# Attention scores as single float32 products from q and k as loaded, the last 64 keys as a chunk of their own, value products in two halves

## Chip, cores and metric

The kernel runs on one core of one Trainium2 chip. The metric is the device time of one execution in microseconds; lower is better. The time before is the median of three runs, and one further execution was profiled.

## What is computed

Sigmoid attention over 4 batches of 12 heads, 448 positions and 64 dimensions, whose output feeds two feed-forward layers with 1792 tokens:

```python
scores = scale * np.matmul(q, k.transpose(0, 1, 3, 2)) - np.log(S)   # S = 448, scale = 1 / 8
attn = 1.0 / (1.0 + np.exp(-scores))
out = np.matmul(attn, v)                       # (4, 12, 448, 64) -> x: (1792, 768)
xn = x / sqrt(mean(x * x) + 1e-06) * rms_g
y = (silu(xn @ w_gate) * (xn @ w_val)) @ w_out     # 768 -> 1536 -> 768
h = y @ w_in2                                      # 768 -> 2048
result = (h - tanh(h)) @ w_out2                    # 2048 -> 768
```

All inputs are float32.

## The kernel before, in words

Heads are worked on in 24 pairs (6 pairs in each of 4 batches). The two heads of a pair lie one above the other on the 128 partitions, 64 rows each, as 64 is the head's dimension. The 448 keys of a head are cut into chunks of 128, 128, 128 and 64.

`pair_load` (L444) brings a pair's q and k (with 4 to 8 transfers on SP's queue, L457) and its v (L466, or L476 and L477 with a fill of zeros on POOL at L471). `pair_prep` (L481) then splits q and k: a copy (L488, recorded at the helper's L278) makes a high part of type float32r, and a subtraction (L489) the low part. `scores` (L500) multiplies, for each chunk and each head, high by high, low by high and high by low (the matmul at L512); head 0 lies in rows 0 to 63 of the array and head 1 in rows 64 to 127. The sum comes out in a PSUM bank for each chunk and head. `sigmoid` (L521) takes each bank through ScalarE into SBUF (L522). `pair_qk` (L527) is called twice for a pair, for the chunks 0 and 1 and for 2 and 3. The short chunks of both heads are put into one tile of 128 rows.

`pair_av` (L541) multiplies with the values: for three chunks and two heads a float32 matmul (L551) whose heads lie in different columns of the array, and one matmul over the whole array (L555) for the short chunks of both heads at once, against a v tile in which the other head's rows are zero. `pair_end` (L561) copies the sum out of PSUM, and `x_end` (L567) squares it (L569) and adds it up (L576) for the norm.

After attention the kernel runs the two feed-forward layers for batches 0 and 1 and then for 2 and 3, as products of float32r parts (L768 and L803). Some of the first of these products are put between attention units of the last batches, with Silu (L712) on ScalarE.

The order is not written out by hand. Each step is added to a list with its engines, a cost for each, its reads, its writes and, for transfers, a time until they land. `Plan.issue` (L81) then simulates the engines with these costs: among the steps that can finish within 300 ns of the soonest it takes the one that was added first (some later work has its rank put back), and every engine gets its steps in the order of the simulated starts. Steps of the stream "attention" keep their order on TensorE. Buffers belong to pools with a cap for each kind: 74 `unit` tiles of 128 x 448 (L243), nine `wt` tiles for weights (L245: `raw` up to 3, `op` up to 6, `whl` and `again` up to 3), three `vs` tiles for v, and eight PSUM banks. `get_ready` (L817) prepares the next pair and loads the one behind it. Before the first scores TensorE runs 16 matmuls on zeros (L285, called at L839).

Of the kernel before, what the change touches and what calls it, by code (L numbers as in the profile page):

```python
# [8 lines left out]
F32 = mybir.dt.float32  # L9
F32R = mybir.dt.float32r  # L10
# [49 lines left out]
class Plan:  # L60
# [153 lines left out]
def tile_sigmoid_attention_moe_moe(  # L214
# [25 lines left out]
    dram_p = ctx.enter_context(tc.tile_pool(name="spill", bufs=1, space=DRAM))  # L240

    plan = Plan({
        "unit": (N_UNIT, {"moe": N_MOE, "s": 14, "qk": 8, "qkr": 4, "acc": 6, "st": 4, "sum": 6, "x": 16, "xr": 4, "tmp_m": 6, "tmp_a": 4, "sq": 3, "rstd": 2,  # L243
                          "xs": 42, "tmp_s": 4, "tmp_x": 4}),
        "wt": (N_WT, {"raw": N_RAW, "whl": 3, "again": 3, "op": 6}),  # L245
        "cv": (N_CV, {"cv": N_CV}),
        "vs": (3, {"vs": 3}),
        "ps": (8, {"mm": 6, "at": 8, "av": 2, "nm": 1, "m2": 8}),
# [3 lines left out]
    def slot(kind, pool, shape, dt, tag):  # L252
        return Slot(kind, lambda: pool.tile(shape, dt, tag=tag, name=tag))
# [4 lines left out]
    def unit(kind, dt=F32):  # L258
        return slot(kind, unit_p, [P, S], dt, "unit")
# [8 lines left out]
    def act(n, psum=False, ptr=False):  # L268
        return {"ACT": ((155 if psum else 195) + n / 1.2, False)}
# [7 lines left out]
    def copy(engines, to, of, reads, writes):  # L277
        add(engines, lambda e: (nc.scalar.copy if e == "ACT" else nc.vector.tensor_copy)(to(), of()), reads, writes)  # L278
# [159 lines left out]
                lambda: two(g[1], 0, ("S3", "S4")), lambda: two(g[1], 1, ("A22",))]  # L438


    qkr_t, vs_t, pair_t, a_t, av_t = {}, {}, {}, {}, {}
    xs, sqs, rcs, rstd, spilled = {}, {}, {}, {}, {}

    def pair_load(b, p):  # L444
        if (b, p) in qkr_t or (b, p) in pair_t:
            return
        t = qkr_t[b, p] = {w: unit("qkr") for w in "kq"}

        def load(w, lo, hi, key):

            for i in range(2):
                rows = slice(i * D, (i + 1) * D)
                of = qkt[b * H + 2 * p + i][rows]
                at = lo + S * (w == "k")
                if w == "k" and lo == 3 * P and b < PAIRED:
                    at += i * D
                add({"SP": (1.4 * (hi - lo), False)}, lambda e, of=of, rows=rows, at=at: nc.sync.dma_start(  # L457
                    out=t[w].tile[rows, lo:hi], in_=of[:, at:at + hi - lo]), [], [t[w][key, lo, i]], after=2000)

        for w, lo, hi in (("k", 0, P), ("q", 0, S), ("k", P, 3 * P), ("k", 3 * P, S)) if (b, p) == (0, 0) else (  # L460
                ("k", 0, 3 * P), ("k", 3 * P, S), ("q", 0, S)) if b < PAIRED else (("k", 0, S), ("q", 0, S)):
            load(w, lo, hi, "t")
            t.setdefault(w + "in", []).extend(t[w]["t", lo, i] for i in range(2))
        v = vs_t[b, p] = slot("vs", vs_p, [P, 4, 2, D], F32, "vs")
        if b < PAIRED:
            add({"SP": (700, False)}, lambda e: nc.sync.dma_start(out=v.tile, in_=vp[b * HP + p]), [], [v["t", i] for i in range(2)], after=2000)  # L466
            return

        def fill(e):
            for i in range(2):  # L470
                nc.gpsimd.memset(v.tile[(1 - i) * D:(2 - i) * D, 3, i, :], 0.0)  # L471

        add({"POOL": (250, True)}, fill, [], [v["t", 0], v["t", 1]])
        for i in range(2):
            def two(e, i=i, of=vt[(b - PAIRED) * H + 2 * p + i], rows=slice(i * D, (i + 1) * D)):
                nc.sync.dma_start(out=v.tile[:, :3, i, :], in_=of[:, :3])  # L476
                nc.sync.dma_start(out=v.tile[rows, 3, i, :], in_=of[rows, 3])  # L477

            add({"SP": (900, False)}, two, [], [v["t", i]], after=2000)

    def pair_prep(b, p):  # L481
        t = qkr_t.pop((b, p))
        f = pair_t[b, p] = {w: unit("qk", F32R) for w in ("kh", "qh", "kl", "ql")}

        def part(w, lo, hi, to):
            h, l, r = f[w + "h"], f[w + "l"], t[w]
            of = [x for x in t[w + "in"] if lo <= x[1][1] < hi]
            copy({**act(hi - lo), **dve(hi - lo, fast=True)}, lambda: h.tile[:, lo:hi], lambda: r.tile[:, lo:hi], of, [h[to]])  # L488
            add({**pool(hi - lo), **dve(hi - lo, psum=False)}, lambda e: ENG[e].tensor_sub(  # L489
                l.tile[:, lo:hi], r.tile[:, lo:hi], h.tile[:, lo:hi].bitcast(F32)), [*of, h[to]], [l[to]])  # L490

        if (b, p) == (0, 0):
            part("k", 0, P, 0)
            part("q", 0, S, 0)
            part("k", P, S, 1)
        else:
            for w in "kq":
                part(w, 0, S, 0)

    def scores(b, p, cs):  # L500

        f = pair_t[b, p]
        ps = {(i, c): bank("at") for c in cs for i in range(2)}
        key = (lambda c: min(c, 1)) if (b, p) == (0, 0) else (lambda c: 0)

        def run(e):
            for c in cs:
                n = min(P, S - c * P)
                for w, q in (("kh", "qh"), ("kl", "qh"), ("kh", "ql")):
                    for i in range(2):  # L510
                        rows = slice(i * D, (i + 1) * D)
                        nc.tensor.matmul(  # L512
                            ps[i, c].tile[:n, :S], lhsT=f[w].tile[rows, c * P:c * P + n], rhs=f[q].tile[rows, :],
                            start=(w, q) == ("kh", "qh"), stop=q == "ql")

        add({"PE": (3 * len(cs) * MM + 200, False)}, run,
            [x for c in cs for x in (f["kh"][key(c)], f["kl"][key(c)])] + [f["qh"][0], f["ql"][0]],
            [x["t"] for x in ps.values()], stream="attention")
        return ps

    def sigmoid(ps, n, to, at=0, key="t"):  # L521
# [3 lines left out]


    def pair_qk(b, p, cs):  # L527
        ps = scores(b, p, cs)
        for c in cs:
            if c < 3:  # L530
                for i in range(2):
                    t = a_t[b, 2 * p + i, c] = unit("s")
                    sigmoid(ps[i, c], P, t)
            else:

                t = a_t[b, p] = unit("s")
                for i in range(2):
                    sigmoid(ps[i, c], D, t, i * D, i)
                pair_t.pop((b, p))

    def pair_av(b, p):  # L541

        ps, v = bank("av"), vs_t.pop((b, p))
        av_t[b, p] = ps
        two = [[a_t.pop((b, 2 * p + i, c)) for i in range(2)] for c in range(3)]
        end = a_t.pop((b, p))

        def halves(e):
            for c in range(3):
                for i, a in enumerate(two[c]):  # L550
                    nc.tensor.matmul(  # L551
                        ps.tile[i * D:(i + 1) * D, :S], lhsT=v.tile[:, c, i, :], rhs=a.tile, start=(c == 0), stop=False)

        def whole(e):
            nc.tensor.matmul(  # L555
                ps.tile[:, :S], lhsT=v.tile[:, 3].rearrange("p i d -> p (i d)"), rhs=end.tile, start=False, stop=True)

        add({"PE": (12 * MM + 150, False)}, halves, [v["t", 0], v["t", 1], *[a["t"] for x in two for a in x]], [ps["t"]], stream="attention")
        add({"PE": (4 * MM, False)}, whole, [v["t", 0], v["t", 1], end[0], end[1]], [ps["t"]], stream="attention")

    def pair_end(b, p):  # L561
        ps = av_t.pop((b, p))
# [253 lines left out]

    def get_ready(at):  # L817
        if at < len(pairs):
            pair_prep(*pairs[at])
            for x in pairs[at + 1:at + 2]:  # L820
                pair_load(*x)

    def attn_units(b):
        units = []
        for at in range(b * HP, (b + 1) * HP):
            units.append(lambda at=at: pair_qk(*pairs[at], (0, 1)))
            if at:
# [13 lines left out]
    nc.gpsimd.memset(expo, -0.5)  # L841


    for p in range(2):
        pair_load(0, p)
    add({"SP": (100, False)}, lambda e: nc.sync.dma_start(out=g_sb, in_=rms_g))
    add({"SP": (100, False)}, lambda e: nc.sync.dma_start(out=id_sb, in_=ident))
    pair_prep(0, 0)
    def x_units(bs, again):
        units = []  # L850
        for i in range(KM // 2):
# [135 lines left out]
```

## Time and profile before

| what | us |
| --- | --- |
| median of three runs | 1117.16 |
| lowest and highest | 1115.34, 1117.31 |
| the profiled execution | 1116.87 |
| its span, first to last instruction | 1115.1 |
| TensorE busy (PE) | 1092.7, 98% |
| VectorE busy (DVE) | 747.9, 67% |
| ScalarE busy (ACT) | 521.5, 47% |
| GpSimd busy (POOL) | 153.4, 14% |

PE is TensorE's matmuls and PEld its weight loads, which run beside them; SPq is the queue in which SP issues transfers. A matmul's record lasts longer than the time it keeps the array, as matmuls are pipelined; the time from the start of one group to the start of the next tells what a group costs. The share of a busy engine over the whole span mixes the attention stage (to about 190 us) and the projections behind it.

### The profile page before, as it was taken

The numbers are of one execution on the slowest core, as the hardware profiler recorded it, in microseconds if no ns is written. First come the engines' busy times: TensorE is split into PE (matmuls) and PEld (weight loads), VectorE is DVE, ScalarE is ACT, GpSimd is POOL, SyncE is SP. The second block draws the span as 40 slices with busy tenths as digits, with TensorE's granted clock in tenths as the row PEclk, the third lists the DMA queues.
The fourth block names the chain that finished last, engine by engine and source line by source line (L and its number), as shares of the span: only waits on it lengthen the run. The fifth ranks groups of instructions, "written<-read, shape, count | busy, mean of one in ns | idle before, by whom it ended". The sixth has DMA issues, their size and how long they took to land.

```text
span 1115.1 us, 15207 instructions
## 1 busy us (share of the span) xinstructions
PE 1092.7 (98%) x5508; PEld 932.4 (84%) x5508; DVE 747.9 (67%) x1162; ACT 521.5 (47%) x917; POOL 153.4 (14%) x130
## 2 busy tenths in 40 slices
PE   8999999999999998999999999999999999999998
PEld 4555556999999997899998888999899989999997
DVE  3767854877578878878698966632666687474651
ACT  5787786442255346456364543312344353242431
POOL 0010011111021100123132001200021021232100
PEclk9999999999999999999999999999999999999999
DMA  4886343467758645599799653333344134656432
GB/s 130 283 250 196 104 135 130 152 253 275 247 183 277 236 156 199 180 322 367 292 333 324 210 193 125 117 121 132 103 150 162 57 99 150 192 187 201 147 116 100
DMA packets 93051, 211.43 MB, mean 190 GB/s; under 512 B 23216, under 2 KB 60208, under 8 KB 92976
## 3 DMA queue, kind: packets, MB, share of 16 engines
q1 hardware_dynamic: 92976, 210.47, 56.1%
q8 instruction: 43, 0.70, 0.3%
q14 instruction: 32, 0.26, 0.1%
HBM read 137.68 MB, written 72.74 MB: 189 GB/s over the span
## 4 chain that ended last, share of the span: by engine, by line
PE 92%; DVE 3%; ACT 2%; issue 1%; DMA 1%; SPq 1%; ACTq 0%; DVEq 0%
PE ps L768 43%; PE ps L803 37%; PE ps L512 5%; PE ps L551 5%; PE ps L555 2%; SPq L457 1%; DVE unit L278 1%; DVE wt L349 1%; ACT wt L278 1%; DVE unit L669 1%; DMA vs<-in_vt 1%; DVE unit L742 0%; PE ps L610 0%; DVE unit L715 0%; PE ps L588 0%
## 5 line engine op out<-in xcount | busy, mean ns | idle before, releaser
L768 PE MATMUL ps<-unit,wt 128*128 128x448 f32 x2520 | 526.9, 368 | 9.0 <-DVE unit L742 4.9
L768 PEld LDWEIGHTS ps<-unit,wt 128*128 128x128 f32 x2520 | 472.0, 188 | 58.5 <-DVE unit L742 6.4
L803 PE MATMUL ps<-unit,wt 128*128 128x448 f32 x2016 | 415.2, 366 | 1.1 <-ACT wt L278 1.1
L803 PEld LDWEIGHTS ps<-unit,wt 128*128 128x128 f32 x2016 | 378.2, 188 | 34.2 <-ACT wt L278 1.5
L278 ACT COPY unit<-ps 128x448 f32<-128x448 f32 x172 | 91.3, 534 | 320.9 <-PE ps L803 200.5
L278 DVE COPY unit<-ps 128x448 f32<-128x448 f32 x80 | 49.9, 624 | 124.8 <-PE ps L803 118.6
L349 DVE TENSOR_TENSOR wt<-cv,wt 128x768 fp32r<-128x768 f32 (+1 forms) x108 | 100.0, 932 | 16.8 <-ACT wt L278 15.2
L522 ACT ACTIVATE unit<-ps 128x448 f32<-128x448 f32 x192 | 91.0, 541 | 6.1 <-PE ps L512 5.1
L278 ACT CAST wt<-cv 128x768 fp32r<-128x768 f32 (+1 forms) x91 | 70.5, 781 | 40.9 <-DVE cv L338 17.1
L669 DVE TENSOR_TENSOR unit<-unit 128x448 fp32r<-128x448 f32 x96 | 77.6, 808 | 9.6 <-ACT unit L278 7.0
L349 POOL TENSOR_TENSOR wt<-cv,wt 128x768 fp32r<-128x768 f32 (+1 forms) x28 | 52.5, 1875 | 194.0 <-ACT wt L278 102.0
L278 ACT CAST unit<-unit 128x448 fp32r<-128x448 f32 (+1 forms) x112 | 62.4, 566 | 30.7 <-DVE unit L715 8.9
L278 DVE CAST unit<-unit 128x448 fp32r<-128x448 f32 (+1 forms) x133 | 59.2, 445 | 25.2 <-DMA unit<-in_qkt 19.9
L512 PE MATMUL ps<-unit 64*128 64x448 f32 (+1 forms) x576 | 70.2, 379 | 5.1 <-DVE unit L278 2.8
L349 POOL TENSOR_TENSOR wt<-wt 128x768 fp32r<-128x768 f32 (+1 forms) x21 | 36.6, 1745 | 269.9 <-ACT wt L278 189.2
L742 DVE TENSOR_TENSOR unit<-ps,unit 128x448 f32<-128x448 f32 x84 | 52.0, 620 | 32.3 <-PE ps L768 22.6
L512 PEld LDWEIGHTS ps<-unit 64*128 64x128 f32 (+1 forms) x576 | 49.1, 172 | 28.8 <-issue 15.7
L338 DVE SCALAR_TENSOR_TENSOR cv<-wt,zero 128x768 uint32<-128x768 uint32 x68 | 67.4, 991 | 4.5 <-DMA wAg<-cv 2.5
L278 ACT CAST wt<-wt 128x768 fp32r<-128x768 f32 (+1 forms) x60 | 44.8, 754 | 53.9 <-PE ps L768 38.1
L551 PE MATMUL ps<-unit,vs 128*64 128x448 f32 x288 | 60.4, 555 | 1.3 <-ACT unit L522 1.3
L278 ACT CAST zero<-wt 128x768 f16<-128x768 bf16 x46 | 49.7, 1081 | 21.4 <-DVE cv L338 14.9
L349 DVE TENSOR_TENSOR wt<-wt 128x768 fp32r<-128x768 f32 (+1 forms) x59 | 51.4, 880 | 6.3 <-ACT wt L278 5.4
(55 smaller groups left out, 599.0 us busy)
## 6 DMA issues: line engine op xcount, KB each, us to landing
wt<-in_w_out SPq DMA_DIRECT2D x28, 768.0 KB, 5.2
sumD<-unit SPq DMA_DIRECT2D x72, 224.0 KB, 2.9
unit<-sumD SPq DMA_DIRECT2D x72, 224.0 KB, 4.8
wt<-in_w_in SPq DMA_DIRECT2D x16, 768.0 KB, 6.0
wC<-cv SPq DMA_DIRECT2D x32, 384.0 KB, 3.9
wt<-wC SPq DMA_DIRECT2D x16, 768.0 KB, 4.5
wt<-in_w_gate SPq DMA_DIRECT2D x12, 768.0 KB, 5.7
wt<-in_w_val SPq DMA_DIRECT2D x12, 768.0 KB, 5.0
```

Of the source, the lines that this page charges most:

```text
L278: add(engines, lambda e: (nc.scalar.copy if e == "ACT" else nc.vector.tensor_copy)(to(), of()), reads, writes)
L338: add(dve(NW, psum=False), lambda e: nc.vector.scalar_tensor_tensor(out=c.tile.bitcast(U32), in0=r.tile[:, :NW, 1], scalar=13, in1=z.tile, ...
L349: add({**dve(n, psum=False), **pool(n)}, lambda e: ENG[e].tensor_sub(lo(), of(), hi().bitcast(F32)), [*reads, *kh], [*kl])
L457: add({"SP": (1.4 * (hi - lo), False)}, lambda e, of=of, rows=rows, at=at: nc.sync.dma_start(out=t[w].tile[rows, lo:hi], in_=of[:, at:at + ...
L512: nc.tensor.matmul(ps[i, c].tile[:n, :S], lhsT=f[w].tile[rows, c * P:c * P + n], rhs=f[q].tile[rows, :], start=(w, q) == ("kh", "qh"), sto ...
L522: add(act(S, psum=True), lambda e: nc.scalar.activation(to.tile[at:at + n, :S], ps.tile[:n, :S], AF.Sigmoid, bias=-math.log(S), scale=1.0 ...
L551: nc.tensor.matmul(ps.tile[i * D:(i + 1) * D, :S], lhsT=v.tile[:, c, i, :], rhs=a.tile, start=(c == 0), stop=False)
L555: nc.tensor.matmul(ps.tile[:, :S], lhsT=v.tile[:, 3].rearrange("p i d -> p (i d)"), rhs=end.tile, start=False, stop=True)
L669: add({**pool(S), **dve(S, psum=False)}, lambda e: ENG[e].tensor_sub(c["l"].tile, t.tile, c["h"].tile.bitcast(F32)), [t["t"], kh], [kl])
L742: add(dve(S), lambda e: nc.vector.tensor_add(t.tile, ps.tile[:, :S], t.tile), [ps["t"], t["t"]], [t["t"]])
L768: nc.tensor.matmul(ps.tile[:, :S], lhsT=part(a), rhs=x[b].tile, start=n in ((1, 2, 5) if opening else (1, 5)) and i == 0 and q == 0, stop= ...
L803: nc.tensor.matmul(ps.tile[:, :S], lhsT=wt, rhs=a[p].tile, start=first and i == 0 and k < GR[ph], stop=last and i == 2, skip_group_check=True)
```

## The change

Scores become one float32 matmul for each chunk and head, straight from q and k as loaded; `pair_prep` and its casts, subtractions and tiles are gone. q and k of a pair come in one transfer on SP (for the first pair in two, the second on ACT's queue) into a tile of the pool `wt`, up to four of them. Three pairs are loaded at the start, and pair `at + 3` is loaded where pair `at + 1` was prepared. The last 64 keys of each head get a tile of 64 rows of their own; v needs no zeros there, and its last chunk lies in rows 0 to 63 for both heads. The value products are eight float32 matmuls, added as two steps of two chunks each. For the first pair the scores are added chunk by chunk. The cap of the kind `s` (sigmoid tiles) goes from 14 to 18; the kinds `qk` and `qkr` leave the pool `unit`.

```diff
-        "unit": (N_UNIT, {"moe": N_MOE, "s": 14, "qk": 8, "qkr": 4, "acc": 6, ...
-        "wt": (N_WT, {"raw": N_RAW, "whl": 3, "again": 3, "op": 6}),
+        "unit": (N_UNIT, {"moe": N_MOE, "s": 18, "acc": 6, ...
+        "wt": (N_WT, {"raw": N_RAW, "qkr": 4, "whl": 3, "again": 3, "op": 6}),
...
     def pair_load(b, p):
...
+        t = qkr_t[b, p] = slot("qkr", wt_p, [P, S + 4 * P], F32, "wt")
+        both = qkt[b * H + 2 * p:b * H + 2 * p + 2].rearrange("h r c -> (h r) c")[D:D + P]
+        end = S + 4 * P if b < PAIRED else 2 * S
+        for e, lo, hi in (("SP", 0, S + P), ("ACT", S + P, end)) if (b, p) == (0, 0) else (("SP", 0, end),):
+            add({e: (650, False)}, lambda e, lo=lo, hi=hi: ENG[e].dma_start(out=t.tile[:, lo:hi], in_=both[:, lo:hi]),
+                [], [t[lo // (S + P)]], after=2000)
+        v = vs_t[b, p] = slot("vs", vs_p, [P, 4, 2, D], F32, "vs")
...
+        if b < PAIRED:
+            at = b * HP + p
+            part(2, lambda: v.tile[:, :3], vp[at, :, :3])
             for i in range(2):
+                part(i, lambda i=i: v.tile[:D, 3, i, :], vp[at, i * D:(i + 1) * D, 3, i, :])
+        else:
+            for i in range(2):
+                part(i, lambda i=i: v.tile[:, :, i, :], vt[(b - PAIRED) * H + 2 * p + i])
...
-    def pair_prep(b, p):
...
     def scores(b, p, cs):
...
-                for w, q in (("kh", "qh"), ("kl", "qh"), ("kh", "ql")):
-                    for i in range(2):
-                        rows = slice(i * D, (i + 1) * D)
-                        nc.tensor.matmul(
-                            ps[i, c].tile[:n, :S], lhsT=f[w].tile[rows, c * P:c * P + n], rhs=f[q].tile[rows, :],
-                            start=(w, q) == ("kh", "qh"), stop=q == "ql")
...
+                for i in range(2):
+                    rows = slice(i * D, (i + 1) * D)
+                    at = S + c * P + (i * D if c == 3 and b < PAIRED else 0)
+                    nc.tensor.matmul(ps[i, c].tile[:n, :S], lhsT=t.tile[rows, at:at + n], rhs=t.tile[rows, :S], start=True, stop=True)
+
+        parts = (0,) if (b, p) != (0, 0) or cs == (0,) else (0, 1)
+        add({"PE": (2 * len(cs) * 375 + 150, False)}, run, [t[x] for x in parts], [x["t"] for x in ps.values()], stream="attention")
...
     def pair_av(b, p):
...
-        def whole(e):
-            nc.tensor.matmul(
-                ps.tile[:, :S], lhsT=v.tile[:, 3].rearrange("p i d -> p (i d)"), rhs=end.tile, start=False, stop=True)
...
+                        ps.tile[i * D:(i + 1) * D, :S], lhsT=v.tile[:n, c, i, :], rhs=a[c][i].tile[:n, :], start=(c == 0), stop=(c == 3))
+
+        for cs in ((0, 1), (2, 3)):
+            add({"PE": (4 * 375 + 75, False)}, lambda e, cs=cs: run(e, cs),
+                [*(v[x] for x in range(3 if b < PAIRED else 2)), *[x["t"] for c in cs for x in a[c]]], [ps["t"]], stream="attention")
...
     def get_ready(at):
         if at < len(pairs):
-            pair_prep(*pairs[at])
-            for x in pairs[at + 1:at + 2]:
-                pair_load(*x)
+            pair_load(*pairs[at])
...
-            units.append(lambda at=at: (get_ready(at + 1), pair_qk(*pairs[at], (2, 3))))
+            units.append(lambda at=at: (get_ready(at + 3), pair_qk(*pairs[at], (2, 3))))
...
-    for p in range(2):
+    for p in range(3):
         pair_load(0, p)
...
-    pair_prep(0, 0)
```

## Rows read from the trace of the kernel before

**Rows 1.** The page's first part: busy time, share of the span and instructions of each engine.

```profile
PE 1092.7 (98%) x5508; PEld 932.4 (84%) x5508; DVE 747.9 (67%) x1162; ACT 521.5 (47%) x917; POOL 153.4 (14%) x130
```

**Rows 2.** Busy time by window: PE, PEld, DVE, ACT, POOL, granted clock, DMA share, GB/s.

```profile
25.00:50.00 25.00, 25.00 (x166) 13.70 (x164) 17.60 (x32) 20.47 (x44) 0.00 (x0) 1.00 0.86 280
```

**Rows 3.** Timeline of PE, one pair: start us, length us, line, count.

```profile
60.05 2.73 PE L512 MATMUL ps<-unit 64*128 64x448 f32 x24
62.71 2.48 PE L551 MATMUL ps<-unit,vs 128*64 128x448 f32 x12
65.12 1.02 PE L555 MATMUL ps<-unit,vs 128*128 128x448 f32 x2
66.07 2.73 PE L512 MATMUL ps<-unit 64*128 64x448 f32 x24
```

**Rows 4.** Timeline of the weight loads, inside the second row above.

```profile
63.14 0.14 PEld L551 LDWEIGHTS ps<-unit,vs 128*64 128x64 f32 x2 [0.23 <-issue]
...
63.89 0.14 PEld L551 LDWEIGHTS ps<-unit,vs 128*64 128x64 f32 x2 [0.23 <-issue]
```

**Rows 5.** The chain that ended last, longest piece: start us, length us, what.

```profile
192.25 51.59 PE ps L768 x252
```

**Rows 6.** Timeline of PE where a pair's scores come in two halves.

```profile
123.08 1.49 PE L512 MATMUL ps<-unit 64*128 64x448 f32 x12
124.50 3.31 PE L768 MATMUL ps<-unit,wt 128*128 128x448 f32 x15
127.74 1.50 PE L512 MATMUL ps<-unit 64*128 64x448 f32 x12
129.16 2.48 PE L551 MATMUL ps<-unit,vs 128*64 128x448 f32 x12
```

**Rows 7.** Groups on VectorE from 6 to 188 us: count, busy us, mean ns, idle before.

```profile
L489 DVE TENSOR_TENSOR unit<-unit 128x448 fp32r<-128x448 f32 x46 | 30.0, 655 | 2.8 <-ACT unit L278 1.2
L278 DVE CAST unit<-unit 128x448 fp32r<-128x448 f32 x39 | 15.2, 390 | 15.2 <-DMA unit<-in_qkt 14.9
```

**Rows 8.** Timeline of PE at the start; brackets: idle before, what ended it.

```profile
1.94 4.54 PE L285 MATMUL ps<-mark 128*128 128x448 bf16 x16 [1.94 <-POOL mark L834]
6.41 0.87 PE L512 MATMUL ps<-unit 64*128 64x448 f32 x6
7.84 2.43 PE L512 MATMUL ps<-unit 64*128 64x448 f32 x18 [0.56 <-ACT unit L278]
13.04 1.64 PE L512 MATMUL ps<-unit 64*128 64x448 f32 x12 [2.77 <-DVE unit L278]
...
17.97 2.72 PE L512 MATMUL ps<-unit 64*128 64x448 f32 x24
```

**Rows 9.** DMA issues: count, KB each, median us from issue to landing.

```profile
wt<-in_w_in SPq DMA_DIRECT2D x16, 768.0 KB, 6.0
...
unit<-in_qkt SPq DMA_DIRECT2D x72, 112.0 KB, 2.8
```

**Rows 10.** Timeline of SP's queue at the start.

```profile
0.74 5.04 SPq L457 DMA_DIRECT2D unit<-in_qkt  x8
```

**Rows 11.** Timeline of PE at its two waits in the middle of attention.

```profile
112.20 1.49 PE L512 MATMUL ps<-unit 64*128 64x448 f32 x12
...
115.84 0.47 PE L512 MATMUL ps<-unit 64*128 64x448 f32 x2 [1.35 <-ACT unit L278]
...
158.40 2.48 PE L551 MATMUL ps<-unit,vs 128*64 128x448 f32 x12 [1.25 <-ACT unit L522]
```

**Rows 12.** Busy time by window, around the first of them.

```profile
112.00:123.08 11.08, 9.39 (x42) 4.11 (x42) 9.92 (x17) 7.86 (x17) 1.41 (x3) 0.85 0.30 85
```

**Rows 13.** Timeline of ACT before the second.

```profile
154.62 1.28 ACT L712 ACT_TABLE_LOAD   x1
```

**Rows 14.** Groups on ACT from 6 to 188 us.

```profile
L522 ACT ACTIVATE unit<-ps 128x448 f32<-128x448 f32 x144 | 67.9, 544 | 5.5 <-PE ps L512 5.1
```

**Rows 15.** Timeline of PE, the longest wait in the projections.

```profile
430.86 14.59 PE L768 MATMUL ps<-unit,wt 128*128 128x448 f32 x63 [2.08 <-DVE unit L742]
```

More of the change, by code (lines that the diff above doesn't have):

```diff
@@ L242, in tile_sigmoid_attention_moe_moe @@
     plan = Plan({
-        "unit": (N_UNIT, {"moe": N_MOE, "s": 14, "qk": 8, "qkr": 4, "acc": 6, "st": 4, "sum": 6, "x": 16, "xr": 4, "tmp_m": 6, "tmp_a": 4, "sq": 3, "rstd": 2,
+        "unit": (N_UNIT, {"moe": N_MOE, "s": 18, "acc": 6, "st": 4, "sum": 6, "x": 16, "xr": 4, "tmp_m": 6, "tmp_a": 4, "sq": 3, "rstd": 2,
                           "xs": 42, "tmp_s": 4, "tmp_x": 4}),
-        "wt": (N_WT, {"raw": N_RAW, "whl": 3, "again": 3, "op": 6}),
+        "wt": (N_WT, {"raw": N_RAW, "qkr": 4, "whl": 3, "again": 3, "op": 6}),
         "cv": (N_CV, {"cv": N_CV}),
@@ L438, in again_units @@
                 lambda: two(g[1], 0, ("S3", "S4")), lambda: two(g[1], 1, ("A22",))]
-    qkr_t, vs_t, pair_t, a_t, av_t = {}, {}, {}, {}, {}
+    qkr_t, vs_t, a_t, av_t = {}, {}, {}, {}
     xs, sqs, rcs, rstd, spilled = {}, {}, {}, {}, {}
     def pair_load(b, p):
[L445 to L449, printed above, removed]
-            for i in range(2):
-                rows = slice(i * D, (i + 1) * D)
[L453 to L469, printed above, removed]
-            for i in range(2):
-                nc.gpsimd.memset(v.tile[(1 - i) * D:(2 - i) * D, 3, i, :], 0.0)
-        add({"POOL": (250, True)}, fill, [], [v["t", 0], v["t", 1]])
-        for i in range(2):
[L475 to L479, printed above, removed]
@@ L481, in pair_prep @@
-    def pair_prep(b, p):
[L482 to L498, printed above, removed]
+        t = qkr_t[b, p] = slot("qkr", wt_p, [P, S + 4 * P], F32, "wt")
@@ new lines, in pair_load, with part @@
+        both = qkt[b * H + 2 * p:b * H + 2 * p + 2].rearrange("h r c -> (h r) c")[D:D + P]
[4 more added lines that the diff above has]
+        v = vs_t[b, p] = slot("vs", vs_p, [P, 4, 2, D], F32, "vs")
+        def part(key, out, of):
+            add({"SP": (650, False)}, lambda e: nc.sync.dma_start(out=out(), in_=of), [], [v[key]], after=2000)
@@ L500, in scores, with rows_of @@
+        if b < PAIRED:
+            at = b * HP + p
+            part(2, lambda: v.tile[:, :3], vp[at, :, :3])
+            for i in range(2):
+                part(i, lambda i=i: v.tile[:D, 3, i, :], vp[at, i * D:(i + 1) * D, 3, i, :])
+        else:
+            for i in range(2):
+                part(i, lambda i=i: v.tile[:, :, i, :], vt[(b - PAIRED) * H + 2 * p + i])
+    def rows_of(c):
+        return min(P, S - c * P)
     def scores(b, p, cs):
-        f = pair_t[b, p]
+        t = qkr_t[b, p]
@@ L503, in scores @@
         ps = {(i, c): bank("at") for c in cs for i in range(2)}
-        key = (lambda c: min(c, 1)) if (b, p) == (0, 0) else (lambda c: 0)
         def run(e):
             for c in cs:
-                n = min(P, S - c * P)
-                for w, q in (("kh", "qh"), ("kl", "qh"), ("kh", "ql")):
-                    for i in range(2):
-                        rows = slice(i * D, (i + 1) * D)
-                        nc.tensor.matmul(
-                            ps[i, c].tile[:n, :S], lhsT=f[w].tile[rows, c * P:c * P + n], rhs=f[q].tile[rows, :],
-                            start=(w, q) == ("kh", "qh"), stop=q == "ql")
@@ L516, in scores @@
-        add({"PE": (3 * len(cs) * MM + 200, False)}, run,
-            [x for c in cs for x in (f["kh"][key(c)], f["kl"][key(c)])] + [f["qh"][0], f["ql"][0]],
-            [x["t"] for x in ps.values()], stream="attention")
+                n = rows_of(c)
+                for i in range(2):
+                    rows = slice(i * D, (i + 1) * D)
+                    at = S + c * P + (i * D if c == 3 and b < PAIRED else 0)
+                    nc.tensor.matmul(ps[i, c].tile[:n, :S], lhsT=t.tile[rows, at:at + n], rhs=t.tile[rows, :S], start=True, stop=True)
@@ L527, in pair_qk @@
     def pair_qk(b, p, cs):
-        ps = scores(b, p, cs)
-        for c in cs:
-            if c < 3:
+        for some in [(c,) for c in cs] if (b, p) == (0, 0) else [cs]:
+            ps = scores(b, p, some)
+            for c in some:
                 for i in range(2):
                     t = a_t[b, 2 * p + i, c] = unit("s")
[L533 to L539, printed above, removed]
+                    sigmoid(ps[i, c], rows_of(c), t)
     def pair_av(b, p):
@@ L544, in pair_av, with run @@
         av_t[b, p] = ps
[L545 to L550, printed above, removed]
-                    nc.tensor.matmul(
-                        ps.tile[i * D:(i + 1) * D, :S], lhsT=v.tile[:, c, i, :], rhs=a.tile, start=(c == 0), stop=False)
-        def whole(e):
-            nc.tensor.matmul(
-                ps.tile[:, :S], lhsT=v.tile[:, 3].rearrange("p i d -> p (i d)"), rhs=end.tile, start=False, stop=True)
-        add({"PE": (12 * MM + 150, False)}, halves, [v["t", 0], v["t", 1], *[a["t"] for x in two for a in x]], [ps["t"]], stream="attention")
-        add({"PE": (4 * MM, False)}, whole, [v["t", 0], v["t", 1], end[0], end[1]], [ps["t"]], stream="attention")
+        a = [[a_t.pop((b, 2 * p + i, c)) for i in range(2)] for c in range(4)]
+        def run(e, cs):
+            for c in cs:
+                n = rows_of(c)
+                for i in range(2):
+                    nc.tensor.matmul(
+                        ps.tile[i * D:(i + 1) * D, :S], lhsT=v.tile[:n, c, i, :], rhs=a[c][i].tile[:n, :], start=(c == 0), stop=(c == 3))
+        for cs in ((0, 1), (2, 3)):
+            add({"PE": (4 * 375 + 75, False)}, lambda e, cs=cs: run(e, cs),
+                [*(v[x] for x in range(3 if b < PAIRED else 2)), *[x["t"] for c in cs for x in a[c]]], [ps["t"]], stream="attention")
     def pair_end(b, p):
```

## The prediction

> **What bounds the kernel now.** I read the busy row first: TensorE is busy for 98% of the span and no other engine for more than 67% [rows 1]. A share over 1115 us says nothing about a stage, so the next view is a window in the attention stage, which the change touches. There PE is busy for all 25.00 us, ACT for 20.47 and VectorE for 17.60, at full clock [rows 2]. The timeline of PE in the same stage repeats itself: one pair of heads takes 66.07 - 60.05 = 6.02 us, of which 2.66 go to the 24 score matmuls, 2.41 to the 12 instructions of the value products of three chunks and 0.95 to the two of the fourth chunk [rows 3]. No wait stands between them. So in the steady part the price of the change is read from PE alone, and work taken from other engines is worth something only where PE does wait. Beyond about 190 us come the projections, in which the change edits nothing.
>
> **The matmuls: what they cost.** Six value calls (three chunks, two heads) make 12 instructions, so a float32 call is two. Their weight loads come two at a time, 0.375 us apart ((63.89 - 63.14) / 2) [rows 4]: the two heads, in different columns of the array, run at once, and a float32 call of two heads takes two slots of 0.375 = 0.75 us. A float32r matmul costs 51.59 / 252 = 0.205 us in the projections [rows 5]. The scores run two at once as well, the heads in different rows of the array: 12 slots of 0.205 are 2.46 of the 2.66 us, which leaves 0.20 for the switch into this kind of work. Likewise 2.41 - 6 x 0.375 = 0.16 and 0.95 - 2 x 0.375 = 0.20 [rows 3]. A switch therefore costs about 0.19.
>
> After the change a pair has 4 chunks x 2 heads x 2 instructions = 16 for the scores, two at once: 8 slots x 0.375 = 3.00 us, instead of 2.46. The value products have 8 calls, again 16 instructions and 8 slots: 3.00, the same slots as now (6 + 2), but the switch to a whole-array matmul is gone, and one to 64 rows for the short chunk comes in its place. From that chunk to the next scores only the number of columns changes. The trace has such a change: the score half with the chunks 0 and 1 takes 124.50 - 123.08 = 1.42 us, and the half that holds the 64-key chunk takes 129.16 - 127.74 = 1.42 [rows 6]. It costs nothing, so I count two switches a pair: 3.00 + 3.00 + 0.38 = 6.38 us, 0.36 more than 6.02, and for 24 pairs +8.6 us. All of this is on the path, since PE is the bound.
>
> TensorEngine Tiling (Array Packing) of the Trainium skill, section Key Properties, says that a change of the tiling mode, not only of the tile, drains TensorE. By that the return from 64 x 64 to 64 x 128 would cost a switch too, and the sum would be 24 x 0.19 = 4.6 us higher; [rows 6] show no such cost where the scores make the same change.
>
> Bounds. No float32 matmul on 64 rows stands in the trace. Below: every switch at 0.16, 6.32 us a pair, +7.2 in all. Above: the score slots at 2 x 0.205 = 0.41, as float32r runs on the same rows, which adds 8 x 0.035 = 0.28 a pair and makes it +15.3; a third switch alone, 0.19 a pair, makes it +13.2. I take 0.375, because 0.205 is also what float32r costs on the whole array [rows 5]: it belongs to the form, not to the rows.
>
> **What the removed preparation gives back.** The casts and subtractions that made high and low parts (VectorE 30.0 us in 46 subtractions and 15.2 in 39 casts of the attention stage, besides ACT's casts) [rows 7] leave engines that are not the bound; what counts is where PE waited for them.
>
> At the start the first scores run at 6.41, when the 16 fill matmuls end; PE then waits 0.56 us for a cast on ACT and 2.77 for a cast on VectorE, because the second pair's transfers and splits come late [rows 8]. From 6.41 to the third pair's scores at 17.97 pass 11.56 us, and the work in it is 2 x 2.66 + 3.36 = 8.68: 2.88 are lost. After the change scores wait for the transfer alone. It is larger (576 columns x 4 B x 128 = 288 KB); rows for 112 and 768 KB land in 2.8 and 6.0 us [rows 9], so issued at 0.74 like the first transfer now it lands between 3.5 and 6.7: under the fill matmuls, or 0.3 late. The second pair's transfer is the fifth that SP issues; at 5.04 / 8 = 0.63 each [rows 10] it goes out at 3.3 and lands by 9.3, and pair 0 keeps PE until 6.41 + 3.2 = 9.6. I take 2.6 back (1.5 to 2.9).
>
> In the middle the two halves of one pair, three projection matmuls and the value products last from 112.20 to 123.08, 10.88 us [rows 11]. The work is 2 x 1.42 + 3 x 0.205 + 3.36 = 6.81; 4.07 are lost: 1.35 in a wait for ACT's cast, some for VectorE's subtraction, and the rest because the clock fell behind that wait (0.85 granted over the stretch, so part of it ran at the lower level, 1.2 GHz) [rows 12]. Cast and subtraction go. What could be late next are the sigmoids, which stand in ACT's queue between the casts of x; I take 3.3 back (1.5 to 4.1). The third wait, 1.25 us at 158.40, is for a sigmoid [rows 11] that stood behind a 1.28 us table load, with Silu from the projections put between sigmoids [rows 13]. The change does not remove Silu; I take 0.5 (0 to 1.3).
>
> The projections' matmuls come in 13 groups between attention units in this stage; a group of 15 takes 127.74 - 124.50 = 3.24 us [rows 6] against 15 x 0.205 = 3.08, so an interruption costs about 0.2 and all of them 2.6. A plan with fewer waits for casts fills fewer gaps; I take a third, 0.8 (0 to 2.6).
>
> Sum: +8.6 - 2.6 - 3.3 - 0.5 - 0.8 = +1.4.
>
> Edits at nothing: sigmoid counts and lengths stay (8 a pair at 67.9 / 144 = 0.47, so 3.8 us under a PE period of 6.4) [rows 14]; the split of the value products into two halves, and fewer, larger transfers on SP's queue. That queue's cover is three pairs of lead, some 19 us; the second rival has what it costs without.
>
> **How it stands to the runs.** The profiled execution took 1116.87 us, 1.8 more than its span and 0.3 under the median of the three. 1116.87 + 1.4 = 1118.3; I say 1118.
>
> **Rivals.**
> (1) *The heads do not pair from the first slot.* The loop issues both instructions of head 0 before those of head 1. If PE took them strictly in order, the second of head 0 would wait for the first, and a group of n slots would take n + 1: +0.375 for each of 24 to 48 score groups, +9 to +18, so 1127 to 1136. The value products, issued by the same kind of loop, argue against it: 12 instructions fit six slots and 0.16 [rows 3, 4], not seven. That is columns, though, and here it is rows. TensorE: Matmul & The Clock Gate of the Trainium skill, Part 3, The mechanism, says that matmuls start and end in strict program order; [rows 3, 4] do not bear that out for columns. If float32 rows did not overlap at all, 8 more slots a pair would give +72, 1190.
> (2) *Loads starve.* The q and k tiles move to the pool of nine buffers in which raw weights (up to 3) and converted weights (up to 6) lie. If these hold eight, a pair's load can go out only when the scores of the pair before are done; its cover is then the value products, 3.2 us, against 0.63 + 2.8 to 6.0 to land: 0.2 to 3.4 us lost a pair, with two buffers or more nothing. Five to ten pairs would give +5 to +15: 1123 to 1133, slower. Against it: loads come earlier in the plan's rank than weights.
> (3) *Faster.* The waits go whole (2.9 + 4.1 + 1.3), all the interruptions go (2.6), and the sum is 8.6 - 10.9 = -2.3; the new plan also shifts waits in the projections, of which the longest is 2.08 us for a VectorE sum [rows 15]. Two or three such gone: 1110 to 1113. For it: a freer ACT and VectorE run ahead; against it: those sums are not edited.
>
> **How the numbers follow.** Forecast as worked out, 1118 with 1114 to 1123: 0.62. Rival 1: 0.11 (0.02 of it without overlap). Rival 2: 0.09. Rival 3: 0.18. The range 1111 to 1127 holds the forecast's case, most of rival 3 and half of rival 2, and takes in the third switch. About 0.2% (2.2 us) is what a measurement of this kernel can tell from no change. Of the forecast's 0.62, 0.03 lies below that, 0.39 within, 0.20 above; with the rivals: faster 0.20, same 0.40, slower 0.40.
>
> **What would show it.** A pair's period of 6.3 to 6.45 us on PE with 16 + 16 instructions; score loads two at a time, 0.375 apart; no PE wait between 6.41 and the third pair's scores; no clock drop near 115. Wrong would be: score groups over 3.4 us (rival 1 or the slot), PE waits that end with a q and k transfer (rival 2), or a gain that lies beyond 190 us (rival 3).

## The result: 8.5 us slower

| | kernel before | changed kernel |
| --- | --- | --- |
| median, us | 1117.24 | 1125.72 |
| lowest and highest | 1115.34, 1117.37 | 1124.59, 1128.24 |
| the profiled execution, and its span | 1116.87, 1115.1 | 1124.59, 1122.8 |

The ratio is 1.0083, with a 95% interval from 1.0063 to 1.0103: slower, clear of the measurement's uncertainty.

The page's busy row of the changed kernel, answering [rows 1], and the window from 25 to 50 us, answering [rows 2]:

```profile
PE 1105.4 (98%) x5364; PEld 908.4 (81%) x5364; DVE 702.3 (63%) x1070; ACT 504.0 (45%) x896; POOL 155.3 (14%) x113
```

```profile
25.00:50.00 25.00, 25.00 (x120) 7.81 (x116) 16.02 (x25) 17.54 (x37) 0.00 (x0) 1.00 0.82 261
```

VectorE and ScalarE have less to do, as meant (16.02 and 17.54 us in this window instead of 17.60 and 20.47). TensorE, the bound, has 144 matmuls fewer in all and is busy 12.7 us longer.

The timeline of PE, answering [rows 3] and [rows 8] (start us, length us, line, count; L285 are the fill matmuls, L479 the scores, L509 the value products, L723 projections):

```profile
1.94 5.60 PE L285 MATMUL ps<-mark 128*128 128x448 bf16 x16 [1.94 <-POOL mark L787]
7.47 5.13 PE L479 MATMUL ps<-wt 64*128 64x448 f32 x24
12.53 3.38 PE L509 MATMUL ps<-unit,vs 128*64 128x448 f32 x16
...
43.27 3.63 PE L479 MATMUL ps<-wt 64*128 64x448 f32 x16
46.83 3.38 PE L509 MATMUL ps<-unit,vs 128*64 128x448 f32 x16
50.14 3.63 PE L479 MATMUL ps<-wt 64*128 64x448 f32 x16
...
174.52 1.47 PE L723 MATMUL ps<-unit,wt 128*128 128x448 f32 x6
```

A pair takes 50.14 - 43.27 = 6.87 us instead of 6.02: 3.56 for the scores, 3.31 for the values. No row after the first has a bracket, so PE waits for nothing, and only one group of projection matmuls stands between attention units. The waits of PE up to 200 us are these, and the first is the one before the fill:

```profile
PE ps L285 <- POOL mark L787: 1.9, 1, 1.9
```

All the waits of [rows 8] and [rows 11] are gone, and the kernel is slower all the same. The 6.87 is the reason. The weight loads of one pair show what it is made of (a row is a run of loads; the bracket is the idle time of the load path before it):

```profile
42.37 0.20 PEld L509 LDWEIGHTS ps<-unit,vs 64*64 64x64 f32 x4 [0.70 <-ACT unit L486]
43.27 0.30 PEld L479 LDWEIGHTS ps<-wt 64*128 64x128 f32 x4 [0.70 <-issue]
44.23 0.19 PEld L479 LDWEIGHTS ps<-wt 64*64 64x64 f32 x4 [0.65 <-issue]
45.12 0.30 PEld L479 LDWEIGHTS ps<-wt 64*128 64x128 f32 x4 [0.71 <-ACT unit L486]
45.61 0.19 PEld L479 LDWEIGHTS ps<-wt 64*128 64x128 f32 x2 [0.18 <-ACT unit L486]
45.98 0.19 PEld L479 LDWEIGHTS ps<-wt 64*128 64x128 f32 x2 [0.18 <-issue]
46.83 0.20 PEld L509 LDWEIGHTS ps<-unit,vs 128*64 128x64 f32 x4 [0.65 <-ACT unit L486]
```

Within one kind of work loads come two at a time, 0.37 us apart, after 0.18 of idle: that is the slot of the prediction, now on 64 rows. But where the shape of the tile changes, the loads pause for 0.65 to 0.71. Chunk 2 of the scores (64 x 128, two slots, 0.75 of work) takes from 43.27 to 44.23, 0.96; the short chunk (64 x 64) from 44.23 to 45.12, 0.89; chunks 0 and 1 of the next pair (four slots, 1.50) from 45.12 to 46.83, 1.71; the short chunk of the values from 42.37 to 43.27, 0.90. Each change costs 0.14 to 0.21 us, and a pair has five, not two.

### The profile page after: what moved, and what is told of

Same layout as the page of the kernel before. It is cut to its first block, busy times and chain, and to the rows that moved or that the text cites. A ratio compares the mean times of both kernels' runs of the same rounds, so it can differ in the third digit from the quotient of the medians.

```text
span 1122.8 us, 14591 instructions
## 1 busy us (share of the span) xinstructions
PE 1105.4 (98%) x5364; PEld 908.4 (81%) x5364; DVE 702.3 (63%) x1070; ACT 504.0 (45%) x896; POOL 155.3 (14%) x113
## 4 chain that ended last, share of the span: by engine, by line
PE 91%; DVE 4%; ACT 1%; DMA 1%; issue 1%; POOL 0%; SPq 0%; DVEq 0%; POOLq 0%; ACTq 0%
PE ps L723 41%; PE ps L758 35%; PE ps L479 8%; PE ps L509 7%; DMA wC<-cv 1%; DVE wt L349 1%; DVE unit L278 1%; ACT unit L278 1%; PE ps L285 1%; DVE unit L624 1%; ACT wt L278 0%; DVE unit L697 0%; DVE unit L589 0%; DVE unit L670 0%; PE ps L543 0%
## 5 line engine op out<-in xcount | busy, mean ns | idle before, releaser
L723 PE MATMUL ps<-unit,wt 128*128 128x448 f32 x2520 | 521.7, 366 | 10.0 <-DVE unit L697 5.2
L723 PEld LDWEIGHTS ps<-unit,wt 128*128 128x128 f32 x2520 | 471.3, 188 | 56.4 <-DVE unit L697 6.8
L278 ACT CAST wt<-cv 128x768 fp32r<-128x768 f32 (+1 forms) x97 | 75.0, 781 | 44.0 <-DVE cv L338 18.8
L479 PE MATMUL ps<-wt 64*128 64x448 f32 (+1 forms) x384 | 86.9, 568 | 0.0
L509 PE MATMUL ps<-unit,vs 128*64 128x448 f32 (+1 forms) x384 | 81.2, 551 | 0.0
L624 DVE TENSOR_TENSOR unit<-unit 128x448 fp32r<-128x448 f32 x94 | 75.5, 804 | 7.3 <-ACT unit L278 4.6
L479 PEld LDWEIGHTS ps<-wt 64*128 64x128 f32 (+1 forms) x384 | 28.5, 172 | 55.8 <-issue 33.7
L349 POOL TENSOR_TENSOR wt<-cv,wt 128x768 fp32r<-128x768 f32 (+1 forms) x25 | 48.3, 1932 | 177.3 <-ACT wt L278 87.8
L509 PEld LDWEIGHTS ps<-unit,vs 128*64 128x64 f32 (+1 forms) x384 | 23.1, 135 | 54.1 <-issue 34.6
L278 ACT CAST zero<-wt 128x768 f16<-128x768 bf16 x50 | 54.1, 1082 | 28.3 <-DVE cv L338 17.0
L278 ACT CAST unit<-unit 128x448 fp32r<-128x448 f32 x95 | 53.5, 567 | 25.0 <-DVE unit L670 9.0
L584 DVE TENSOR_TENSOR unit<-unit 128x448 fp32r<-128x448 f32 x82 | 51.8, 643 | 6.1 <-ACT unit L278 4.7
```

Source lines behind the costliest of these rows:

```text
L349: add({**dve(n, psum=False), **pool(n)}, lambda e: ENG[e].tensor_sub(lo(), of(), hi().bitcast(F32)), [*reads, *kh], [*kl])
L479: nc.tensor.matmul(ps[i, c].tile[:n, :S], lhsT=t.tile[rows, at:at + n], rhs=t.tile[rows, :S], start=True, stop=True)
L509: nc.tensor.matmul(ps.tile[i * D:(i + 1) * D, :S], lhsT=v.tile[:n, c, i, :], rhs=a[c][i].tile[:n, :], start=(c == 0), stop=(c == 3))
L584: add({**pool(S), **dve(S, psum=False)}, lambda e: ENG[e].tensor_sub(t["l"].tile, of.tile, t["h"].tile.bitcast(F32)), [of["t"], kh], [kl])
L624: add({**pool(S), **dve(S, psum=False)}, lambda e: ENG[e].tensor_sub(c["l"].tile, t.tile, c["h"].tile.bitcast(F32)), [t["t"], kh], [kl])
L723: nc.tensor.matmul(ps.tile[:, :S], lhsT=part(a), rhs=x[b].tile, start=n in ((1, 2, 5) if opening else (1, 5)) and i == 0 and q == 0, stop= ...
```

## Experiments

Each is timed beside the kernel before on the same chip, e1 to e4 on one chip and e5 to e8 on another; the kernel before itself came to 1117.2 to 1118.8 beside them, so ratios compare better than medians. "A pair" is the period of one pair of heads in the steady part, in us. "Attention" is the time in us from the first score matmul to the start of the last value matmul in the profiled execution, less 0.2045 us for each projection matmul that stands between them (the cost of [rows 5]). It holds three of the sums for the norm (0.7 to 0.9 us each), in the changed kernel, e1, e2 and e6 only two, and two or three single fill matmuls of 0.29 us.

| kernel | median | ratio to before, 95% | a pair | attention |
| --- | --- | --- | --- | --- |
| before | 1117.2 to 1118.8 | 1 | 6.02 | 162.0 |
| changed | 1125.7 | 1.0083 (1.0063 to 1.0103) | 6.87 | 168.6 |
| e1, wide scores | 1117.5 | 0.9995 (0.9986 to 1.0005) | 6.52 | 161.7 |
| e2, short chunk first | 1119.0 | 1.0008 (0.9999 to 1.0018) | 6.50 | 161.9 |
| e3, wide scores and values | 1116.9 | 0.9990 (0.9981 to 1.0000) | 6.36 | 162.5 |
| e4, before with the values alone | 1125.5 | 1.0062 (1.0039 to 1.0085) | 5.96 | 169.1 |
| e5, e3 unmixed | 1113.8 | 0.9960 (0.9945 to 0.9975) | 6.36 | 158.5 |
| e6, changed with idle splits | 1123.5 | 1.0050 (1.0033 to 1.0066) | 6.87 | 168.6 |
| e7, before unmixed | 1117.0 | 0.9985 (0.9976 to 0.9994) | 6.02 | 163.8 |
| e8, e5 with 8 fill matmuls | 1112.4 | 0.9945 (0.9931 to 0.9960) | 6.36 | 159.5 |

**e1: no score matmul of 64 columns.**

```diff
-        end = S + 4 * P if b < PAIRED else 2 * S
+        end = S + 4 * P
...
-                    nc.tensor.matmul(ps[i, c].tile[:n, :S], lhsT=t.tile[rows, at:at + n], ...
+                    nc.tensor.matmul(ps[i, c].tile[:, :S], lhsT=t.tile[rows, at:at + P], ...
```

The sigmoid of the short chunk then reads the 64 rows of the sum that hold its keys.

> The changed kernel, but the scores of the 64-key chunk are formed with 128 columns of k (the 64 keys and 64 columns of zeros), so that no score matmul has 64 columns. Same number of matmuls and slots. Theory (each change between 128 and 64 columns of float32 matmuls costs TensorE a switch of 0.15 to 0.21 us, two a pair inside the scores): the scores of a pair take 3.21 instead of 3.56 us, a pair's period 6.51 instead of 6.86, and the run 24 x 0.35 = 8.4 us less than 1125.7: 1117.3. Rival (the group is longer because its matmuls wait for PSUM banks or sigmoids around the short chunk): the same 3.56 and 1125.7. Rival (no other row of the scores matters and the loss is elsewhere, in transfers or the projections): under 2 us of change.

Its timeline of PE (L478 scores, L508 values):

```profile
68.42 3.28 PE L478 MATMUL ps<-wt 64*128 64x448 f32 x16
71.63 3.38 PE L508 MATMUL ps<-unit,vs 128*64 128x448 f32 x16
74.94 3.28 PE L478 MATMUL ps<-wt 64*128 64x448 f32 x16
```

The scores take 71.63 - 68.42 = 3.21 us, the values 3.31 as in the changed kernel. The same number of matmuls, with more weight columns, is 0.35 us a pair faster, and the run is at 1117.5 where 1117.3 was expected: 8.2 us under the changed kernel, nearly all of the 8.5 us of loss. (Its attention stage is only some 7 us shorter in the profiled execution, because it holds a wait of 1.1 us for a sigmoid that the changed kernel does not have.)

**e2: the same matmuls in another order.**

```diff
-            for c in cs:
+            for c in (cs[::-1] if cs == (2, 3) else cs):
```

> The changed kernel with one edit of order: in the step with the chunks 2 and 3 the short chunk is multiplied first. Nothing is added or taken away. On TensorE the scores of chunk 3 then follow the value products of chunk 3, both with 64 rows and 64 columns. Theory (the cost is in changes of the array's division): five changes a pair become three, 2 x 0.175 us less a pair, a period of 6.51 and 1117.3 for the run. Rival (a 64-column float32 matmul is slow by itself, or waits for its banks): the count of such matmuls is unchanged, so 1125.7; and since the sigmoids of chunk 2 come later, possibly 1 to 2 us more.

```profile
59.30 3.00 PE L509 MATMUL ps<-unit,vs 128*64 128x448 f32 x14
61.72 0.59 PE L479 MATMUL ps<-wt 64*64 64x448 f32 x1
62.13 0.54 PE L509 MATMUL ps<-unit,vs 64*64 64x448 f32 x2
62.15 3.72 PE L479 MATMUL ps<-wt 64*64 64x448 f32 x15
65.80 3.00 PE L509 MATMUL ps<-unit,vs 128*64 128x448 f32 x14
```

A pair takes 6.50 us. Nothing was added or removed; the 64 x 64 matmuls of the values and of the scores now stand side by side, so closely that the first score matmul starts before the last value matmuls do. The rival, that a 64-column float32 matmul is slow by itself, falls. The run came to 1119.0, 1.7 more than expected, with an attention stage like e1's; its first scores start at 7.93 in the profiled execution, e1's at 7.16.

**e3: both products on full tiles, the two changes a pair that the prediction counted.**

```diff
-                n = rows_of(c)
                 for i in range(2):
                     nc.tensor.matmul(
-                        ps.tile[i * D:(i + 1) * D, :S], lhsT=v.tile[:n, c, i, :], rhs=a[c][i].tile[:n, :], ...
+                        ps.tile[i * D:(i + 1) * D, :S], lhsT=v.tile[:, c, i, :], rhs=a[c][i].tile, ...
```

with e1's edit, and v of every pair laid out with zeros in the other head's rows and brought by one transfer.

> The changed kernel with the short chunk on 128 columns in the scores and on 128 rows in the value products (sigmoids of 128 rows, v with zeros in the other head's rows, for all pairs one transfer of v). Every score matmul is then 64 rows x 128 columns and every value matmul 128 rows x 64 columns: two changes a pair, as the prediction counted. Theory: a period of 8 x 0.375 + 0.21 + 8 x 0.375 + 0.15 = 6.36 us, 24 x 0.50 = 12 us less than the changed kernel: 1113.7, which is 3.5 under the kernel before. Rival (the switch to 64 rows was free, only columns count): 1117.3, as with wide scores alone. Rival (the larger v transfers or the plan bring waits): above 1117.

Its timeline of PE (L467 scores, L496 values, L710 projections), first the steady part, then a later one:

```profile
59.60 3.28 PE L467 MATMUL ps<-wt 64*128 64x448 f32 x16
62.81 3.23 PE L496 MATMUL ps<-unit,vs 128*64 128x448 f32 x16
65.96 3.28 PE L467 MATMUL ps<-wt 64*128 64x448 f32 x16
...
122.64 1.77 PE L467 MATMUL ps<-wt 64*128 64x448 f32 x8
124.34 2.10 PE L710 MATMUL ps<-unit,wt 128*128 128x448 f32 x9
126.37 1.77 PE L467 MATMUL ps<-wt 64*128 64x448 f32 x8
```

65.96 - 59.60 = 6.36 us, to the hundredth what was expected. The run was not: 1116.9 instead of 1113.7. The later rows say where it went. The planner put 12 groups of projection matmuls between attention units, where e1 has one, and its attention stage is 162.5, where a period of 6.36 would make about 158.

**e5: e3 without those groups.**

```diff
                 if stream and streams[stream][stream_at[stream]] != n:
                     continue
+                if stream == "moe" and stream_at["attention"] < len(streams["attention"]):
+                    continue
```

> The kernel with wide scores and wide values (e3), with one line more in the planner: no product of the projections starts before the last attention step. In e3, whose period is the 6.36 us that was expected, 12 groups of projection matmuls stand between attention units, and from its first score to its last value product, less 0.2045 us for each of those matmuls, pass 162.5 us; e1, with one such group and a period longer by 0.15, needs 161.7. Theory (an interruption costs about 0.35 us, in switches and in scores that come in two halves): 162.5 becomes 158.2 and the run 1112.5. Rival (the interruptions fill time in which attention would wait, and cost nothing): 1116.5 to 1117.5, with new waits on TensorE before 165 us.

```profile
60.47 3.28 PE L469 MATMUL ps<-wt 64*128 64x448 f32 x16
63.67 3.23 PE L498 MATMUL ps<-unit,vs 128*64 128x448 f32 x16
66.83 3.28 PE L469 MATMUL ps<-wt 64*128 64x448 f32 x16
```

The same period, an attention stage of 158.5, and 3.1 us less for the run. One fill matmul of 0.3 us now stands behind the stage, so the groups cost (162.5 - 158.5 - 0.3) / 12 = 0.31 us each. The rival, that the groups fill time in which attention would wait, falls for this kernel: PE has no wait between the first score and 200 us, and only one group of scores is longer than the others, by 0.4 us. It is 0.4% faster than the kernel before.

**e7: the same line in the kernel before.**

> The kernel before with the planner's line of e5: no product of the projections before the last attention step. Its 13 groups between attention units go, which were part of what the change gave back. Theory (an interruption costs about 0.35 us): 4 us less, 1113.5 to 1114.5. Rival (they fill gaps in which the scores would wait for casts): 1117 to 1119, with the projections' 19 us of work moved behind and waits in attention instead.

The waits of PE up to 200 us (total, times, longest):

```profile
PE ps L514 <- ACT unit L280: 3.5, 3, 2.2
PE ps L514 <- DVE unit L280: 3.0, 1, 3.0
```

By the attention stage the rival was right. L280 is the cast of q and k in this kernel; without projection matmuls to fill in, the scores wait longer for it (6.5 us, where the kernel before has 4.7 for casts), and the stage is 163.8 instead of 162.0. The run agrees only in part: it was 1.8 us faster than the kernel before by the medians, where the theory expected 4 and the rival nothing. The profiled execution is one of three in ten with a granted clock of 0.993, the others having 0.995 to 0.997, so its stage is longer than that of most; where the gain lies stays open.

**e4: the value products alone, in the kernel before.** `pair_av`, the sigmoid tiles and the loads of v as in the changed kernel; `pair_prep` and the three float32r products of the scores as before.

> The kernel before with the value products alone changed: tiles of 64 rows for the last keys, eight float32 matmuls in two steps, v loaded as in the changed kernel; q and k still split, scores still three float32r products. Theory: the value products take 3.30 to 3.36 us as before (8 slots either way, one switch for another), float32r scores show no cost at 64 columns, so the run is 1115 to 1117.5, no difference that counts. Rival (the value products carry part of the loss): 1119 or more.

Timeline of PE (L511 scores, L545 values), then of VectorE:

```profile
28.68 3.38 PE L545 MATMUL ps<-unit,vs 128*64 128x448 f32 x16
31.99 2.73 PE L511 MATMUL ps<-unit 64*128 64x448 f32 x24
34.64 3.38 PE L545 MATMUL ps<-unit,vs 128*64 128x448 f32 x16
...
49.87 1.49 PE L511 MATMUL ps<-unit 64*128 64x448 f32 x12
54.20 0.70 PE L511 MATMUL ps<-unit 64*128 64x448 f32 x4 [2.85 <-DVE unit L278]
...
56.97 3.93 PE L545 MATMUL ps<-unit,vs 128*64 128x448 f32 x16
```

```profile
50.37 0.62 DVE L278 CAST zero<-wt 128x768 f16<-128x768 bf16 x1 [5.17 <-DMA wt<-in_w_gate]
...
52.63 0.39 DVE L278 CAST unit<-unit 128x448 fp32r<-128x448 f32 x1
```

The theory was right on the period, 34.64 - 28.68 = 5.96 us (3.31 for the values, 2.65 for the scores), and wrong on the run by 8 us. The scores wait for casts: 3.73 us at the start, 2.85 here, and shorter ones later; after a wait the clock is below full (56.97: 16 value instructions in 3.93 instead of 3.38, at a granted clock of 0.85). The VectorE rows show why. A conversion of weights stood at the head of VectorE's queue and waited 5.17 us for its transfer, and casts of q and k, which the scores need, stood behind it. So what the waits of the kernel before cost, 9.6 us as worked out below, is not fixed: with preparation on the path, an edit that does not touch it nearly doubled that (169.1 - 162.0, and 24 x 0.06 that the shorter period should have saved: 8.5 more). This also shows what undoing the float32 scores alone would bring: nothing.

**e6: the load put back, without the dependency.** The casts and subtractions run again, into tiles that no one reads:

```diff
+    def idle_split(b, p):
+        t = qkr_t[b, p]
...
+            copy({**act(S), **dve(S, fast=True)}, lambda h=h: h.tile, of, parts, [h[0]])
+            add({**pool(S), **dve(S, psum=False)}, lambda e, h=h, l=l, of=of: ENG[e].tensor_sub(
+                l.tile, of(), h.tile.bitcast(F32)), [*parts, h[0]], [l[0]])
```

> The changed kernel with the casts and subtractions of the kernel before put back, 23 pairs x 2 casts and 2 subtractions into tiles that nobody reads: the other engines carry the work again, but no score waits for it. What gave back the 8 us of waits that the kernel before had on TensorE in the attention stage? Theory A (the dependency: scores stood behind transfer, cast and subtraction): no wait returns, 1124.5 to 1127. Theory B (the load on ScalarE, VectorE and their queues): sigmoids and copies come late, waits return, 1129 to 1134.

Groups on VectorE from 6 to 180 us; the idle splits are the two with `wt` on the right:

```profile
L472 DVE TENSOR_TENSOR unit<-wt,unit 128x448 fp32r<-128x448 f32 x46 | 28.0, 623 | 6.4 <-ACT unit L278 5.1
...
L278 DVE CAST unit<-wt 128x448 fp32r<-128x448 f32 x30 | 11.7, 390 | 40.5 <-DMA wt<-in_qkt 40.5
```

The work of [rows 7] is back, and PE still waits for nothing up to 200 us; the attention stage is 168.6 as without it. So it was not the lighter load on ScalarE and VectorE that gave the waits for casts back. But the edit keeps the changed kernel's transfers, one for a pair and three pairs ahead, so it does not set the missing casts apart from q and k that come earlier. The trace of the kernel before does so in part. At the start a cast ended the longest wait, and it had itself waited for a transfer:

```profile
12.50 0.39 DVE L278 CAST unit<-unit 128x448 fp32r<-128x448 f32 x1 [0.98 <-DMA unit<-in_qkt]
```

What came back there is owed to transfers that come earlier. At the wait that ends at 115.84 the transfers had been issued by 104.6, and ScalarE's cast (0.56 us, from 115.23) stood behind other casts and sigmoids in its queue; that wait is owed to the missing cast. The wait for a sigmoid at 158.40 [rows 11] had another reason: it stood behind a table load for Silu, and in the changed kernel the first such load comes at 184.61, behind the stage. The run is even 2.2 us under the changed kernel's median; its attention stage is the same, so that lies beyond it, and its cause stays open.

**e8: half the fill.** e5 with `N_WARM = 8`.

> e5 with 8 fill matmuls instead of 16. In the changed kernel the first transfer of q and k lands 3.6 us after its issue at 0.74, at 4.3, and TensorE runs fill matmuls until 7.5. Theory: the scores start at about 4.9 at the lower clock, and 1 to 1.5 us are won against e5, 1111 to 1111.5. Rival (the clock rises no earlier, and the first scores at half speed cost what the start wins): within 0.5 of e5.

```profile
1.94 3.17 PE L286 MATMUL ps<-mark 128*128 128x448 bf16 x8 [1.94 <-POOL mark L776]
5.04 4.98 PE L469 MATMUL ps<-wt 64*128 64x448 f32 x24
...
25.84 4.38 PE L469 MATMUL ps<-wt 64*128 64x448 f32 x16
30.23 3.23 PE L498 MATMUL ps<-unit,vs 128*64 128x448 f32 x16
```

```profile
28.52 0.62 DVE L279 COPY unit<-ps 128x448 f32<-128x448 f32 x1
```

The scores start at 5.04 instead of 7.66. The attention stage is 1.0 us longer than in e5, and 1.4 us remain by the medians. Only 0.2 of the 1.0 is the clock: the first 24 score matmuls, which start before it has risen, take 4.91 us instead of 4.71. The other 0.8 lie in one group of scores, 30.23 - 25.84 = 4.39 us instead of e5's 3.59 (3.20 in the steady part), whose last matmuls start at 29.19, when VectorE's copy of an earlier sum out of PSUM has ended (the VectorE row). At 0.9945 (0.9931 to 0.9960) it is the fastest of all, 0.55% under the kernel before.

## Why the prediction came out as it did

The measured 1125.7 lies in the range, 1111 to 1127, at its upper end, and slower was given as much chance as no difference. The forecast, 1118 with 1114 to 1123, missed by 7.7 us. That the time lies in the range at all is luck: the term that failed passed its own upper bound, and with no more given back than was predicted the run would have come to 1118 + 11.8 = 1130. Step by step:

- *TensorE is the bound of the stage, and other engines' work is worth only the waits that it causes.* Right: e6 put the work back, and the attention stage did not move.
- *A float32 call of two heads takes two slots of 0.375 us, also on 64 rows.* Right, and it was the step without a row: 16 + 16 instructions, loads two at a time, 0.37 apart. The upper bound of 0.41 a slot and rival 1 (strict order, or no overlap) fall: in e3 8 slots and one switch are 3.21 us, and a ninth slot would have made it 3.58. In the compiled program the two instructions of one head stand behind each other, and still the loads come in pairs and the group fits eight slots. TensorE: Matmul & The Clock Gate of the Trainium skill, Part 3, The mechanism, says that matmuls start in strict program order; these rows do not agree with it.
- *"It costs nothing, so I count two switches a pair."* This is the step that failed. [rows 6] showed a chunk of 64 columns at no cost, but in float32r. As float32 the same chunk costs a switch when it begins and another when it ends, 0.35 us a pair together (e1, e2). The return from the short chunk of the values to the scores, a change of columns again, costs one more, 6.52 - 6.36 = 0.16 (e1, e3). That makes five instead of two. In the compiled programs the float32r matmul of 64 columns still names the whole width of the array, and the float32 one names half of it, though the rows call both 64*64. That fits the missing cost, but no run sets the type and the named width apart. A shape was carried from one type to another. The term measured 24 x (6.87 - 6.02) = +20.4 us, for +8.6 predicted and +15.3 as its upper bound. TensorEngine Tiling (Array Packing) of the Trainium skill, Key Properties, on draining at each change of the mode, agrees with every one of the five pauses; I had set it aside for a row of another type.
- *What comes back.* Mis-sized the other way. First, the work at the start was counted wrong: the prediction took two pairs of scores, 2 x 2.66, but [rows 8] have 6 + 18 + 12 = 36 score matmuls there, one and a half pairs. The work was 18 x 0.205 + 0.20 + 3.36 = 7.25 us, and 4.31 of the 11.56 were lost, not 2.88. The three waits then went whole: 4.31 at the start, 4.07 with the clock and 1.25 at the sigmoid are 9.6, for 6.4 taken. The attention stage grew by 168.56 - 162.02 = 6.5 us, so 20.4 - 6.5 = 13.9 left it: the 9.6; 1.0 for a norm sum (0.71) and a fill matmul (0.29) that stood at 134.66 and 164.11 and now come behind the stage; and 3.3 with the interruptions, 12 fewer than before, about 0.27 each. e5 measured 0.31. I had priced one at 0.2 from the switch alone, and one that splits a pair's scores into two halves costs another: 1.42 + 3.24 + 1.42 - 2.66 - 3.08 = 0.34 by [rows 6]. I took a third of them where nearly all went.
- *The start.* The scores begin at 7.47 instead of 6.41, which no step foresaw; by the spread shown below it need not be the change's doing.
- *Rival 2, loads that starve in the pool of weights.* No wait of PE ends with a transfer of q and k.
- *Rival 3.* Its condition came true, all waits and nearly all interruptions gone. With the two switches that were predicted it would nearly have been right, 1110 to 1113: e5 is that kernel, at 1113.8.

The sum had two errors of opposite sign: 11.8 us too little for the switches, and 5.7 too little given back (9.6 + 3.3 for 7.2). Of the 7.7 us by which the profiled span grew, 6.5 lie in the attention stage, 1.06 ahead of it and 0.1 behind it, where the norm sum and the fill matmul now stand.

## What to carry to other kernels

When matmuls of different shapes follow each other, count the changes of tile shape, and price one from a row of the same type: padding a short chunk to the full tile, or placing equal shapes side by side, bought 7 to 8 us here for no extra matmul (e2, e1). A preparation step that stands between a transfer and TensorE costs what stands ahead of it in its engine's queue, not its own length, so 4.07 us hung on a cast of 0.56 here, and doing such work again beside the path cost nothing (e6). Filling gaps with other matmuls pays only while there are gaps.

## What the runs showed that I had not expected

The 16 fill matmuls are the same in nine of the ten profiled kernels, and the scores behind them start anywhere from 6.41 (the kernel before) to 7.93 us (e2). The spacing tells why: 448 columns every 0.373 us are 1.2 GHz, every 0.189 us 2.4 GHz, and the rise came after 7 of them in the kernel before, after 13 in the changed one and after all of them in e2, whose 16 take 7.93 - 1.93 = 6.00 us:

```profile
1.93 6.07 PE L285 MATMUL ps<-mark 128*128 128x448 bf16 x16 [1.93 <-POOL mark L787]
```

The clock column of the window table shows 1.00 throughout this stretch, so the start must be read from the spacing. A difference of 1 us at the start of two profiles is no finding about the kernels.
